# Output projection moved from the attention runs to a dense final stage of seven half-size products per pair of row tiles

## The chip, the cores and the metric

The kernel runs on one core of one Trainium2 chip. The metric is the device time of one execution in microseconds. A core has five engines, each working through its own instructions in order: TensorE (PE; its weight loads are listed apart as PEld), VectorE (DVE), ScalarE (ACT), GpSimd (POOL) and SyncE (SP). They are kept in step by semaphores. DMA transfers are issued from the instruction streams of SP, ACT and POOL; an issue whose data is not ready holds up everything behind it in that stream. Matrix products land in PSUM, eight banks of 128 x 512 fp32, from which DVE or ACT must take them before a bank can be written again.

## The reference

```python
def reference(A_x, A_k_cache, A_v_cache, A_wq, A_wo, B_x, B_w_gate, B_w_up, B_w_down):
    def _A_ref(x, k_cache, v_cache, wq, wo):      # 32 heads of 192, 2048 cached keys
        W = min(4096, max(256, Sk // 4))          # 512: the last 512 keys are used
        q = (x @ wq) as (B, Hq, Sq, Dh)
        k, v = the last W rows of k_cache, v_cache
        p = softmax((q @ k^T) * Dh ** -0.5)
        o = p @ v                                 # (B, Hq, Sq, Dh)
        return o as (B, Sq, Hq * Dh) @ wo         # 6144 -> 640
    def _B_ref(x, w_gate, w_up, w_down):          # F = 1536
        return (sigmoid(x @ w_gate) * (x @ w_up)) @ w_down
    xn = layernorm(A_x)                           # 2048 rows of 640
    s = _A_ref(xn, A_k_cache, A_v_cache, A_wq, A_wo)
    g = silu(_B_ref(xn, B_w_gate, B_w_up, B_w_down))
    return A_x + s * g
```

All inputs and the output are bf16. (Shortened to what is computed; `as` stands for the transposes and reshapes.)

## The kernel before

The order of every instruction on every engine is written out by hand, as the order of the statements of the program. It has two parts.

**The GLU** (L250 to L528) goes over the 2048 rows in four quarters s of 512. The f loop (L442) has twelve steps: ten products of gate and up into a double bank of PSUM (L449), the sigmoid on ACT (L454), the product with up on DVE into hT_sb (L455). Four double banks are used in turn (bank2, L79), so TensorE can be some tiles ahead of ACT and DVE. Then four row tiles q go through w_down (L495, products L499), with a sigmoid on ACT (L506) and a product on DVE (L507); the finished gate is stored to DRAM from POOL's queue (gB_d, L523). Layernorm, its transposes and sums of x stand between these steps.

Beside that the GLU stage finds a scale for wq: its 16 pieces are loaded (scan_load, L168), their magnitudes are folded into a running maximum on DVE (scan_fold, L177; L181 and L183). In quarter 2, at f = 6, set_scale (L185) reduces it on DVE (L186), writes the 128 numbers to DRAM (mx_d, L188) and reads them back into every partition (mx_row, L189), both from POOL's queue; at f = 11 set_scale2 (L191) makes the scale, a power of two. Quarter 3 then makes the query weights: scale_w (ACT: L219, copies L224) and sum_w (differences on DVE, L237 to L241). The query product is done by seven products in place of eight, on halves of 64 rows, in fp16 and bf16; that is what the scale and the sums are for.

**The runs** (loop L778): 16 runs r = (pi, g), where pi is a half of the rows (1024) and g a group of two pairs of heads (8 groups). Even runs have pi = 0, odd ones pi = 1. A run has

- 16 score tiles (stage_s, L647; products L655; exponential on ACT, L659), in two double banks, with the next run's query products between them (query_slots L573, q_after L776; products L565, copies on DVE L586, sums on DVE L603);
- 8 PV tiles (stage_pv, L661; products L673; DVE reciprocal L679, DVE product into o_st L680). Two of them fill one o_st, which SP's queue then transposes by DMA into oT (L686). There are two buffers of o_st (ost_pool, L535); in run 0 four slices of acc_lo stand in for them (L666), in run 15 there are four.
- after each PV tile one row tile of the output projection of the *previous* run (stage_wo, L738; wo_mm, L711; L716): six chunks of 128, each with 512 and with 128 columns, added on DVE to an fp32 sum acc (L747). With the last group the sum is multiplied by the gate, x is added, and the row tile is stored (finish, L722; gate and x are prepared on POOL, L708 and L709, as acc times gate plus x). The last run's eight projections come after the loop (L844).

k is loaded from POOL's queue (load_k, L131), scaled on DVE (L142) and transposed from SP's queue (L146); v is loaded from ACT's queue at the end of odd runs (L839), wo from ACT's queue (L556). The raw parts of wq come on POOL's queue (L202); their scaling and copies are on ACT, their differences on DVE, within PV of the even runs.

## Time and profile before

| | us |
|---|---|
| Median of 3 runs | 903.48 (903.33 to 903.51) |
| Profiled execution, span from the first to the last instruction | 901.5 |
| GLU, first quarter and its preparation, to 47.48 | 47.48 |
| GLU quarters 1 to 3 with their down parts, 47.48 to 164.30 | 116.82 |
| Query products of run 0, 164.30 to 175.64 | 11.34 |
| Run 0, scores, then PV, to 208.80 | 22.40, 10.76 |
| Runs 1 to 14, to 848.90 | 640.10 |
| Run 15 and the last projections, to 897.35 | 48.45 |
| After the last matmul | 4.15 |

The stage borders are read from the first and last instructions of each stage in the timeline. In the tables by stretch, a row gives the stretch, its length, then for each engine the busy time (and the number of instructions), the clock that TensorE was granted (1.00 is full), the share of time that the DMA engines were busy, and GB/s. In the page's second part, each digit is the busy share in tenths of one 40th of the span (22.5 us). In a group's line the two figures behind the bar are the busy time in all and the mean ns of one. In a line of the queue of an engine (POOL and SP among them), the bracket is the wait ahead of the instruction and what ended it.

### The profile page before, as it was taken

How to read it: one execution, taken by the hardware profiler on the slowest of the kernel's cores; microseconds unless marked ns; L12 is line 12 of the kernel's file. 1: busy time of each engine (PE TensorE's matmuls, PEld its weight loads, DVE VectorE, ACT ScalarE, POOL GpSimd, SP SyncE). 2: the span in 40 equal slices, each digit the busy share in tenths (PEclk: the TensorE clock that was granted, in tenths of full speed). 3: DMA queues.
4: the chain of work that ended last, by engine and by line, in shares of the span. 5: the costliest groups of instructions: out<-in, count | busy, mean ns of one | idle time of the engine just before them, and what ended most of it. 6: DMA issues, size and time to landing. Idle time of an engine off the chain costs nothing.

```text
span 901.5 us, 18561 instructions
## 1 busy us (share of the span) xinstructions
PE 895.3 (99%) x7791; PEld 531.9 (59%) x7791; DVE 652.5 (72%) x1093; ACT 432.9 (48%) x511; POOL 179.9 (20%) x222
## 2 busy tenths in 40 slices
PE   9999999999999999999999999999999999999998
PEld 5545454565656565656565656566666656565665
DVE  5879957777677866786778677866786678666567
ACT  4323346754247533753375437642854285424240
POOL 0051212771001100110011001100110000001983
PEclk9999999999999999999999999999999999999999
DMA  9993374415544545363626372727192715263745
GB/s 288 265 267 94 97 147 100 123 53 89 96 82 70 134 79 98 60 143 70 108 57 146 57 119 47 156 54 124 34 169 45 133 21 131 39 121 126 162 127 123
DMA packets 188357, 100.38 MB, mean 111 GB/s; under 512 B 156208, under 2 KB 180656, under 8 KB 188272
## 3 DMA queue, kind: packets, MB, share of 16 engines
q1 hardware_dynamic: 159088, 57.77, 32.1%
q0 software_dynamic: 9408, 29.93, 14.2%
q10 hardware_dynamic: 19776, 11.49, 5.4%
q8 instruction: 61, 1.00, 0.5%
q14 instruction: 24, 0.20, 0.1%
HBM read 57.87 MB, written 5.24 MB: 70 GB/s over the span
## 4 chain that ended last, share of the span: by engine, by line
PE 98%; DVE 1%; DMA 0%; ACT 0%; SPq 0%; issue 0%; POOL 0%; DVEq 0%
PE ps_all L716 23%; PE ps_all L565 20%; PE ps_all L673 19%; PE ps_all L655 18%; PE ps_all L449 11%; PE ps_all L499 6%; PE ps_all L362 1%; DMA x_sb<-in_A_x_dram 0%; ACT E L659 0%; DVE tmp L728 0%; DVE ps_all L725 0%; DVE o_sb L726 0%; SPq L297 0%; DVE stats L324 0%; POOL o_sb L729 0%
## 5 line engine op out<-in xcount | busy, mean ns | idle before, releaser
L659 ACT ACTIVATE E<-ps_all 128x1024 bf16<-128x1024 f32 x256 | 252.8, 1022 | 302.7 <-PE ps_all L655 279.0
L716 PE MATMUL ps_all<-wo_g,oT 128*128 128x512 bf16 (+2 forms) x1542 | 228.3, 299 | 0.0
L655 PE MATMUL ps_all<-qT,kT 64*128 64x512 bf16 x1536 | 194.3, 376 | 0.0
L673 PE MATMUL ps_all<-v_sb,E 128*128 128x193 bf16 x2048 | 189.8, 247 | 0.1
L673 PEld LDWEIGHTS <-E 128*128 128x128 bf16 x2048 | 168.6, 98 | 18.7 <-issue 6.8
L716 PEld LDWEIGHTS <-oT 128*128 128x128 bf16 x1542 | 122.0, 98 | 77.8 <-issue 2.1
L586 DVE COPY qp<-ps_all 128x512 f32<-128x512 f32 x150 | 100.8, 688 | 58.4 <-PE ps_all L565 58.4
L603 DVE TENSOR_TENSOR qT<-ps_all,qp 128x512 bf16<-128x512 f32 x165 | 109.7, 688 | 46.0 <-PE ps_all L565 39.4
L655 PEld LDWEIGHTS <-kT 64*128 64x128 bf16 x1536 | 75.3, 94 | 89.4 <-issue 5.2
L680 DVE TENSOR_TENSOR o_st<-ps_all,rden 128x768 bf16<-128x768 f32 x120 | 114.9, 957 | 5.0 <-DMA oT<-o_st 0.8
L202 POOL DMA_DIRECT2D raw<-in_A_wq_dram x80 | 48.0, 605 | 276.3 <-ACT wB L224 239.0
L135 POOL DMA_DIRECT2D k_sb<-in_A_k_cache_dram x32 | 32.7, 1027 | 270.6 <-DVE o_st L680 151.3
L219 ACT ACTIVATE raw<-raw,w_sc 128x1536 f16<-128x1536 bf16 x37 | 58.3, 1575 | 1.3 <-DMA raw<-in_A_wq_dram 0.4
L499 PE MATMUL ps_all<-wd_sb,hT_sb 128*128 128x512 bf16 (+1 forms) x384 | 52.8, 299 | 0.0
L565 PE MATMUL ps_all<-XB,wB 64*128 64x512 f16 x420 | 52.0, 376 | 0.0
L565 PE MATMUL ps_all<-X,w 64*128 64x512 bf16 x420 | 51.9, 376 | 0.0
L565 PE MATMUL ps_all<-XA,wA 64*128 64x512 f16 x420 | 51.9, 376 | 0.0
L747 DVE TENSOR_TENSOR acc_lo<-ps_all,acc_lo 128x640 f32<-128x640 f32 x48 | 39.5, 823 | 15.3 <-PE ps_all L716 15.0
L455 DVE TENSOR_TENSOR hT_sb<-ps_all,sig_sb 128x512 bf16<-128x512 f32 x48 | 32.4, 682 | 22.2 <-ACT sig_sb L454 11.5
L679 DVE RECIPROCAL rden<-ps_all 128x4 f32<-128x4 f32 x128 | 23.1, 181 | 33.5 <-PE ps_all L673 32.4
L454 ACT ACTIVATE sig_sb<-ps_all 128x512 bf16<-128x512 f32 x48 | 28.0, 596 | 40.1 <-PE ps_all L449 37.1
L747 DVE TENSOR_TENSOR acc_hi<-ps_all,acc_hi 128x640 f32<-128x640 f32 x48 | 39.3, 819 | 7.8 <-PE ps_all L716 7.8
(118 smaller groups left out, 764.4 us busy)
## 6 DMA issues: line engine op xcount, KB each, us to landing
raw<-in_A_wq_dram POOLq DMA_DIRECT2D x80, 192.0 KB, 3.8
k_sb<-in_A_k_cache_dram POOLq DMA_DIRECT2D x32, 192.0 KB, 5.8
wo_g<-in_A_wo_dram ACTq DMA_DIRECT2D x6, 960.0 KB, 6.9
v_sb<-in_A_v_cache_dram ACTq DMA_DIRECT2D x28, 192.0 KB, 3.7
gB_d<-gB_sb POOLq DMA_DIRECT2D x16, 160.0 KB, 4.1
gBa_sb<-gB_d SPq DMA_DIRECT2D x16, 160.0 KB, 3.7
xa_sb<-in_A_x_dram SPq DMA_DIRECT2D x16, 160.0 KB, 3.8
out_dram<-o_sb SPq DMA_DIRECT2D x13, 160.0 KB, 1.8
```

Source lines behind the costliest of these rows:

```text
L219: nc.scalar.activation(raw.bitcast(F16), raw, AF.Copy, scale=w_up)
L449: nc.tensor.matmul(gu[:, i, :], lhsT=w[:, c, f * P:(f + 1) * P], rhs=xnT[s][:, c, :], start=(c == 0), stop=(c == NCD - 1),)
L499: nc.tensor.matmul(oB_ps[:, d0:d0 + dsz], lhsT=hT_sb[:, f, q * P:(q + 1) * P], rhs=wd_sb[:, f, d0:d0 + dsz], start=(f == 0), stop=(f == NF ...
L565: nc.tensor.matmul(ps_all[:, b, :], lhsT=w(r, c), rhs=x[r, c, :], start=(first and k == 0), stop=(k == len(cs) - 1), skip_group_check=True,)
L586: nc.vector.tensor_copy(dst, part(b))
L603: nc.vector.tensor_tensor(q_out(i, u, pp), part(b), t, ALU.add)
L655: nc.tensor.matmul(ps[:, b, :], lhsT=kT[h, c * PC + j, :], rhs=qT_t[r][i, j][h, pp, :], start=(j == 0), stop=(j == PC - 1),)
L659: nc.scalar.activation(E_t[r, i, pp][:, c, :, :], ps, AF.Exp, scale=scale_qk)
L673: nc.tensor.matmul(o_ps[:, q // 2, q % 2, 0:DH + 1], lhsT=E[:, c, h, q * P:(q + 1) * P], rhs=vt[:, c, 0:DH + 1], start=(c == 0), stop=(c = ...
L680: nc.vector.tensor_tensor(o_st[:, :, h * DH:(h + 1) * DH].rearrange("p (b i) d -> p b i d", b=2), o_ps[:, :, :, 0:DH], rden[:].to_broadcas ...
L716: nc.tensor.matmul(oA[:, d0 - base:d0 - base + dsz], lhsT=oT_t[r, i, pp][:, q * PC + j, :], rhs=wo_t[runs[r][1]][:, cc, d0:d0 + dsz], star ...
L747: nc.vector.tensor_tensor(acc[t][:], oA[:, 0:D], acc[t][:], ALU.add)
```

## The change

The projection with wo leaves the runs. stage_wo, wo_mm, finish, load_wo, prepare and the pools for them are gone. Each transposed oT (384 KB) is stored to a DRAM array oT_d instead, from SP's queue (store_o), queued after the next transpose. After run 15 a final stage computes the whole projection. It takes the 6144 rows of wo as two halves h of 24 chunks; for each half and each of 8 pairs of row tiles (rows q of i = 0 and 1) it does seven products of half the size in place of eight (two by two blocks: row tile i, half of the 24 chunks, left or right 320 columns). So there are 16 steps m of 7 products of 12 matmuls with 320 columns, in fp16: 1344 matmuls, where there were 1542 of 512 or 128 columns. Each step loads its four quads (128 x 1536, 384 KB) two steps ahead from SP's queue, scales them on ACT, sums them on DVE (sum_quad), and takes the products out with three copies on ACT (keep) and four results on DVE (result), into acc for h = 0 and, with gate, acc and x, to the output for h = 1. The blocks of wo are loaded (load_ops), scaled on DVE (scale_op) and subtracted on POOL (sum_op): for h = 0 in runs 12 to 14, for h = 1 at m = 1 to 6. POOL prepares gate, acc and x at m = 7 to 14.

Two new scales are needed, for wo and for v. wo is scanned within the GLU: sixteen pieces of 480 KB, each loaded from POOL's queue into one of two buffers, its magnitude taken on ACT and folded on DVE one and two places later (wo_scan), at f 7, 9, 11 and q 1, 3 of quarter 1, f 1 to 11 and q 1, 3 of quarter 2, and f 1 to 9 of quarter 3. Its scale is set in the down part of quarter 3. v is scanned in the runs: magnitudes on ACT in the even runs, maxima on DVE (abs_v, max_v), the last four wholly on DVE in run 14, and its scale set in runs 14 and 15.

Several things move: the weight sums of the later groups go from DVE to POOL and their work is spread over PV of even and odd runs (weights); there are two sets of weight tiles and two k buffers; k is loaded at the start of even runs, and scaled and transposed at the first and fifth PV tile of odd runs; v is loaded from SP's queue; PV takes the banks in the order 0 1 2 3 2 3 0 1; run 15 puts its PV tiles between its score tiles; o_st has two buffers in every run, oT four.

```diff
+        wos_pool = bctx.enter_context(tc.tile_pool(name="wos_pool", bufs=2))
+        def wo_scan(n):
+            ok = range(HQDH // P // UC)
+            if n - 2 in ok and n > 2:
+                nc.vector.tensor_tensor(womax[:], womax[:], wos[n - 2][:], ALU.max)
+            if n in ok:
+                wos[n] = wos_pool.tile([P, UC, D], BF16, name="wos")
+                nc.gpsimd.dma_start(wos[n][:], wo_r[:, n * UC:(n + 1) * UC, :])
+            if n - 1 in ok:
+                nc.scalar.activation(womax[:] if n == 1 else wos[n - 1][:], wos[n - 1][:], AF.Abs)
...
+        wo_scan_at = [(1, f) for f in (7, 9, 11, 13, 15)] + [(2, f) for f in (1, 3, 5, 7, 9, 11, 13, 15)]
+        wo_scan_at += [(3, f) for f in (1, 3, 5, 7, 9)]
...
+                if (s, f) in wo_scan_at:
+                    wo_scan(wo_scan_at.index((s, f)))
                 if (s, f) in folds:
                     scan_fold(wmax, folds[s, f])
...
+                if (s, NF + q) in wo_scan_at:
+                    wo_scan(wo_scan_at.index((s, NF + q)))
+                if s == 3 and q == 0:
+                    set_scale(womax[:].rearrange("p c n -> p (c n)"), mx_row_o, mx_o, 1)
+                elif s == 3 and q == 3:
+                    set_scale2(mx_row_o, mx_o, o_up, o_down)
...
     def stage_pv(r, i, pp, h):
         if h == 0:
-            n, k = TQ * DH, i * G + pp
-            if r == 0:
-                ost_t[0] = lo_flat[:, k * n:(k + 1) * n].bitcast(BF16).rearrange("p (q d) -> p q d", q=TQ)
-            else:
-                ost_t[0] = (late["ost"] if r == last else ost_pool).tile([P, TQ, 2 * DH], BF16, name="o_st")[:]
+            ost_t[0] = ost_pool.tile([P, TQ, 2 * DH], BF16, name="o_st")[:]
...
             nc.sync.dma_start_transpose(oT[:], o_st.rearrange("p q d -> p (q d)"))
-            oT_t[r, i, pp] = oT
+            store_o()
+            oT_t.append((runs[r], i, pp, oT))
+
+    def store_o():
+        while oT_t:
+            (pi, g), i, pp, oT = oT_t.pop()
+            c = (g * G + pp) * PC
+            nc.sync.dma_start(
+                oT_d[pi][i][:, :, c:c + PC, :].rearrange("q p j e -> p q j e"),
+                oT[:].rearrange("p (q j) e -> p q j e", q=TQ),
+            )
...
+    def abs_v(g, n):
+        v = v_t[g, n // 2][n % 2][:, :, 0:DH]
+        a = vmax if (g, n) == (0, 0) else vabs_pool.tile([P, KC, DH], BF16, name="vabs")
+        vabs[g, n] = a
+        if g == NG - 1:
+            nc.vector.tensor_single_scalar(a[:].bitcast(I32), v.bitcast(I32), 0x7FFF7FFF, op=ALU.bitwise_and)
+        else:
+            nc.scalar.activation(a[:], v, AF.Abs)
+
+    def max_v(g, n):
+        if (g, n) != (0, 0):
+            nc.vector.tensor_tensor(vmax[:], vmax[:], vabs.pop((g, n))[:], ALU.max)
...
+            if r == last - 2 and 8 <= k < 12:
+                scale_op(0, (0, 4, 5, 3)[k - 8])
...
+            if pi == 1 and g < NG - 1 and k in (2, 4):
+                max_v(g, k // 2 + 1)
+            if (pi, g) == (0, NG - 1) and k in (6, 7, 8, 9):
+                abs_v(g, k - 6)
+                max_v(g, k - 6)
+            if (pi, g) == (0, NG - 1) and k == 9:
+                set_scale(vmax[:].rearrange("p c n -> p (c n)"), mx_row_v, mx_v, 2)
...
         for k, x in enumerate(pv_list):
+            if pi == 1 and g + 1 < NG and k in (0, 4):
+                scale_k((g + 1, k // 4))
+                turn_k((g + 1, k // 4))
             stage_pv(r, *x)
-            share = (k + 1) * len(wo_list) // len(pv_list)
-            while done < share:
-                stage_wo(*wo_list[done])
-                done += 1
...
+            if pi == 0 and g < NG - 1:
+                if k in (1, 2):
+                    abs_v(g, k - 1)
+                elif k in (4, 6):
+                    max_v(g, k // 2 - 2)
+            if pi == 0 and 1 <= g < NG - 1 and k in (3, 5):
+                weights(g + 1, 3 + k // 5)
+            if pi == 1 and g + 2 < NG and k in (1, 3, 5):
+                weights(g + 2, k // 2)
+        store_o()
+        if pi == 0 and g < NG - 1:
+            for n in (2, 3):
+                abs_v(g, n)
         if pi == 1 and g + 1 < NG:
             for pp in range(G):
-                load_v(g + 1, pp, nc.scalar)
+                load_v(g + 1, pp, nc.sync)
...
-    for i in range(2):
-        for q in range(TQ):
-            stage_wo(last, i, q)
+    for m in range(NP):
+        X, Y, Z = (4, 5, 6) if m % 2 == 0 else (0, 1, 2)
...
+        if m + 2 < NP:
+            load_quads(m + 2)
+        if m == 1:
+            load_ops(1)
+        elif m == 2:
+            for n in (0, 4, 5, 3):
+                scale_op(1, n)
+        elif 3 <= m < 7:
+            sum_op(1, m - 3)
+        if 7 <= m < NP - 1:
+            prep_load(m + 1)
+            prep(m + 1)
+        product(m, Y, "S1", 1, True)
...
+        keep(Y, p5s)
+        product(m, X, "S2", 2, False)
...
+        product(m, Z, "A12", 3, True)
+        result(m, 0, LEFT, Z, p1s)
...
+        product(m, X, "S3", 4, False)
+        result(m, 1, RIGHT, X, p5s)
...
+            product(m + 1, 4 - X, "A11", 0, True)
+            keep(4 - X, p1s)
+        product(m, Y, "S4", 5, False)
+        result(m, 0, RIGHT, Y, u2s)
+        product(m, X, "A22", 6, False)
+        result(m, 1, LEFT, X, None)
```

Here product() is twelve matmuls of 320 columns, keep() a copy on ACT, and scale_quad and sum_quad (left out above) put A21, A11, A22, A12 on ACT and the four sums of the next step on DVE. POOL's part in a step with h = 1 is prep(): gate times the scales, acc times gate, plus x, for both row tiles.

## The prediction

> **What bounds the kernel now.** I read the page's totals and slices first, then its chain, then the stages one by one.
>
> ```profile
> PE 895.3 (99%) x7791; PEld 531.9 (59%) x7791; DVE 652.5 (72%) x1093; ACT 432.9 (48%) x511; POOL 179.9 (20%) x222
> ...
> DVE  5879957777677866786778677866786678666567
> ...
> PE ps_all L716 23%; PE ps_all L565 20%; PE ps_all L673 19%; PE ps_all L655 18%; PE ps_all L449 11%; PE ps_all L499 6%; PE ps_all L362 1%; DMA x_sb<-in_A_x_dram 0%; ACT E L659 0%; DVE tmp L728 0%; DVE ps_all L725 0%; DVE o_sb L726 0%; SPq L297 0%; DVE stats L324 0%; POOL o_sb L729 0%
> ```
>
> TensorE is the bound and never waits; the output projection (L716) is 23% of the chain. But VectorE is at 9 tenths in slices 3 and 4, inside the GLU, where this change adds work. By stage (columns: stretch, length, then busy time of PE, PEld, DVE, ACT, POOL):
>
> ```profile
> 73.38:86.42 13.04, 13.04 (x97) 7.39 (x96) 12.22 (x18) 3.17 (x5) 1.69 (x3) 1.00 0.52 135
> 86.42:112.32 25.90, 25.90 (x121) 11.72 (x120) 23.73 (x38) 9.79 (x15) 6.47 (x10) 1.00 0.37 93
> ...
> 125.36:151.26 25.90, 25.90 (x121) 11.72 (x120) 18.24 (x32) 18.92 (x28) 6.27 (x9) 1.00 0.68 148
> ```
> ```profile
> 198.04:208.80 10.76, 10.76 (x129) 10.60 (x129) 9.09 (x16) 0.97 (x1) 6.35 (x9) 1.00 0.61 100
> 208.80:848.90 640.10, 640.10 (x5952) 389.55 (x5952) 464.85 (x779) 320.43 (x358) 76.87 (x94) 1.00 0.49 93
> 848.90:897.35 48.45, 48.45 (x424) 30.39 (x422) 31.75 (x48) 15.30 (x16) 32.43 (x24) 1.00 0.54 143
> ```
>
> The down part of GLU quarter 1, the f loop of quarter 2 (DVE 92%) and that of quarter 3; then run 0's PV alone (10.76), runs 1 to 14 (45.72 each), run 15 with the last projections.
>
> **The saving.** A row tile of L716 takes 1.63 us in the chain (12 matmuls of 320 columns in the mean: 0.136 each). Eight leave each of runs 1 to 14: 45.72 - 13.04 = 32.68, times 14 is 457.5. Run 15 alone: 16 score tiles at 0.68, PV 10.76, and 1.7 because its first five score tiles now run at the pace of the exponential (1.0 each, L659) with nothing between: 23.4. The final stage: 16 x 7 x 12 matmuls at 0.136 = 182.8. With 4.15 after the last matmul: 208.8 + 457.5 + 23.4 + 182.8 + 4.15 = 876.7, 24.8 below the profiled span of 901.5 (the fp16 and bf16 forms of L565 both take 376 ns, so the type costs nothing). Everything below is added to 876.7.
>
> **The scan of wo in the GLU.** Sixteen POOL loads of 480 KB (those of XA: 4.8 us to landing), 16 Abs of 128x1920 on ACT (from 1575 ns for 1536 and 521 for 384: 0.915 ns an element, so 1.93 us) and 15 maxima on DVE (L183: 1.16). Each engine works in order, and on ACT each Abs stands among the sigmoids and waits for its load; behind it wait the sigmoids, then hT on DVE, then TensorE, which can be three tiles ahead. There are two wos buffers, so load n also waits on POOL until DVE has taken maximum n-2.
>
> ```profile
> 105.09 2.10 DVE L186 TENSOR_REDUCE w_sc<-wmax 128x1 f32<-128x1920 bf16 x1
> ...
> 114.02 0.68 DVE L455 TENSOR_TENSOR hT_sb<-ps_all,sig_sb 128x512 bf16<-128x512 f32 x1
> ```
> ```profile
> 107.49 0.59 POOL L188 DMA_DIRECT2D mx_d<-w_sc  x1 [13.30 <-DVE w_sc L186]
> 115.02 0.56 POOL L189 DMA_DIRECT2D mx_row<-mx_d  x1 [6.95 <-DMA mx_d<-w_sc]
> ```
> ```profile
> 110.78 1.28 ACT L454 ACT_TABLE_LOAD   x1
> 112.07 1.08 ACT L454 ACTIVATE sig_sb<-ps_all 128x512 bf16<-128x512 f32 x2
> ```
>
> Quarter 2: TensorE starts the down products at 112.15 and needs the last hT at 115.1; it comes at 114.70, 0.4 before. The set of the query scale (f 6) keeps POOL 7.5 us between mx_d and mx_row. Behind it now queues wo load 8 (f 7), and Abs 8 stands on ACT ahead of the table load and the sigmoids of f 10 and 11. Five maxima (5.8) come ahead of the reduction on a DVE with no gap there: mx_row 115.0 + 5.8 = 120.8; load 121.4, landed 126.2; Abs to 128.1; table and two sigmoids to 130.5; last hT 131.2. That is 16 us late for a need at 115.1; I take +16. Low end without the 5.8: +10. High, if loads land in 6.6 us, as those of XC: +18.
> By the Trainium skill (DMA: Bandwidth & Descriptors, section Anatomy of one DMA — SWDGE (gpsimd) path) such a write has a fixed cost of about 2 us; mx_d here took 7.2. By the rule this term would be about 11.
>
> Quarter 3: ACT holds 18.92 plus four waits of 1.4 to 1.9 for DVE's weight sums, 25 of 25.9. Abs at f 1 and 3 fall into such waits; those at f 5 and 7 don't (3.86); maxima stand ahead of the sums at f 1, 3 and 9 (3.5). 7.3 less 0.9 of slack: I take +7 (low 0.7, the busy sum 18.92 + 7.72 against 25.9; high 10, if loads hold it too).
>
> wo's scale: L186's 2.1, mx_d 7.5, mx_row 4.2 after the first of the last four down tiles: DVE waits in set_scale2 until about 17 us after that tile's end, ahead of the first query sum, whose bank TensorE wants at 13.0: with the sum's 0.69, +4.5 (2 to 7).
>
> **PV without cover.** In run 0 of the trace PV runs dense and VectorE keeps up, but there o_st is four slices of acc_lo. Now it has two buffers in every run, so the fifth product waits for the first transpose.
>
> ```profile
> 198.04 10.83 PE L673 MATMUL ps_all<-v_sb,E 128*128 128x193 bf16 x128
> ...
> 202.21 9.32 SPq L686 DMA_TRANSPOSE oT<-acc_lo  x4
> ```
> ```profile
> oT<-o_st SPq DMA_TRANSPOSE x60, 4.6
> ```
>
> Counted from PV's start: transpose 0 issued 4.2, landed 8.8; product 4 (7.1 in run 0) ends 9.8, product 5 11.0; transpose 1, issued 6.8, landed 11.4; product 6 ends 12.5. The next run's first query slot wants that bank at 12.06: +0.5 for each of eight runs, 4 in all (landing 3.7: none; 7.0: 2.9 each, 23). In the seven even runs two maxima over v (0.56, from L183's slope) move product 6 to 12.9 and the second maximum to 13.5. The fourth Abs waits for it (two buffers), and ACT runs Abs (0.87) ahead of the next run's exponentials: the first ends at 15.4, and the third score tile, due at 13.1, starts at 15.5: +2.4 each, 17 (10 to 33 by the same landings).
>
> **Covered, or small.** The stores queue behind the next transpose on SP, and the v loads, moved from ACT's queue to SP's, behind the stores; v is needed 15 us later, at the next PV: 0. If that cover went, PV would start late. The stores add 1.57 MB a run; the queue of wo and v (q10) took 48.7 us (5.4% of the span) for 11.49 MB, so about 6.6 us; the DMA engines' 22.4 us a run (0.49 of 45.72), less 2 for wo, become 27 of 32.7: busy, not full. Weight sums on POOL (L237 to L241: 4.2 a chunk, two or three a run): 0. K loads now start in the even run, 25 us ahead of use: 0. In run 13 DVE scales half of wo (four of 128x3840, some 1.2 each by L142's 0.63 for 1536), in run 14 it takes v's last four magnitudes and maxima (4.5); both stand between query sums whose banks TensorE wants again within 2.4 us: +4 (0 to 8, nearly all of the 9.3). In the final stage a pair takes TensorE 84 x 0.136 = 11.4; ACT scales four quads and keeps three products, 4 x 1.58 + 3 x 0.44 = 7.6; DVE takes four sums of 128x1536 (0.96 by L183's slope) and from pair 8 on eleven ops of 128x320 (0.41 to 0.53, L725 and L726), about 9: TensorE leads; at pair 2 DVE waits for the second half of wo behind 1.6 MB of quads: +1.5 (0 to 8). From pair 8 DVE's ops with two SBUF inputs (7.0) meet POOL's 7.6; in run 0 a meeting cost L221 0.23 (0.84 for 0.61). Some eleven a pair are 2.5, just the slack: +5 (0 to 22, if the two never overlapped: 3.2 x 7).
> The Trainium skill (SBUF — State Buffer, section Who interferes with whom) says that they never do: the port pair is locked for a whole instruction. This rule would make it the 22; the row, 0.23, is the nearer.
>
> **Sum.** 876.7 + 16 + 7 + 4.5 + 4 + 17 + 4 + 1.5 + 5 = 935.7; the runs' median stands 2.0 above the profiled span: **938 us**.
>
> **Rivals.** Covered: TensorE works up to three tiles ahead of ACT and DVE, and the scan hides as the query scan does now. For it: not one wait of TensorE inside the GLU. Against it: 0.4 us of slack in quarter 2. All low ends but quarter 2's and the v maxima at nil: 876.7 + 2 + 4 = 883, **faster**; it decides if the added stalls stay under 24.8.
> Late transposes: landings of 7.0 and 8.3 us occur before, beside K loads; at 7.0 the PV terms become 23 + 33: 973. Against: now K loads run outside PV, stores behind.
> The change not done as said: 1344 products of 320 columns are counted in the code; if their pace were that of 98 ns loads plus stream (0.15), 938 + 19 = 957.
>
> **Chances.** Forecast 0.58 (own range 912 to 958); late transposes or slow products 0.14; between the forecast and no change 0.06; covered 0.18 (883, and up to 901 as the low ends are left); within 0.2% (what the measurement can tell from none) 0.04. So faster 0.18, same 0.04, slower 0.78. The range 889 to 962 leaves out the lower half of the covered case and the upper half of the late one, about a tenth on each side.
>
> **What would show it.** In the profile after: waits of PE L449's line and its down products in quarters 2 and 3 for DVE or ACT, 20 to 30 us in all; ACT's Abs waiting on wos loads; DVE's o_st waiting on DMA; score tiles of odd runs waiting for ACT; a final stage of 183 to 190 us with PE dense. Wrong, if PE shows no waits in the GLU, or if the final stage has the largest ones.

## The result: 1034.8 us against a forecast of 938

| | before | after |
|---|---|---|
| Median, us | 903.47 (4 runs, 903.33 to 903.51) | 1034.82 (4 runs, 1029.68 to 1039.98) |
| Span of the profiled execution | 901.5 | 1027.9 |
| TensorE busy | 895.3 | 908.7 |
| Mean granted clock of TensorE | 1.0 | 0.959 |

The changed kernel is slower by a ratio of 1.1454 (95% interval 1.1408 to 1.1500). Slower was forecast, but by 35 us, not by 131; the time lies outside the range of 889 to 962. The profiled execution is the shortest of the four.

First the page of the changed kernel: busy time by engine, then its 40 slices for TensorE and for the clock that it was granted.

```profile
PE 908.7 (88%) x7593; PEld 571.4 (56%) x7593; DVE 727.0 (71%) x1086; ACT 574.7 (56%) x633; POOL 420.2 (41%) x410
...
PE   9999577699989989889899999896989966999886
...
PEclk9999979999999999999999999998999877999989
```

TensorE, busy 99% of the span before, now stands idle for 119 us (1027.9 less 908.7). A slice is 25.7 us: the deep holes are in slices 5 to 8 (the GLU and the query products), 28 (run 13), 33 and 34 (the final stage) and 40, with shallow ones through the runs between, and the clock dips below 9 tenths in four of the deep ones (6, 28, 33 and 34). By stage (columns as in the tables of before) the GLU, the query products of run 0, run 15 and the final stage; then, in a second table, runs 1 to 12 and runs 13 and 14.

```profile
0.00:197.51 197.51, 166.81 (x985) 83.30 (x985) 139.22 (x227) 98.98 (x121) 45.02 (x68) 0.97 0.68 183
197.51:217.00 19.49, 14.85 (x107) 6.43 (x107) 8.99 (x18) 8.33 (x14) 16.98 (x25) 0.82 0.40 98
...
767.20:791.15 23.95, 23.12 (x224) 14.67 (x224) 17.38 (x33) 15.61 (x16) 0.23 (x1) 1.00 0.55 150
791.15:1023.40 232.25, 198.26 (x1347) 135.88 (x1344) 165.63 (x183) 107.74 (x108) 122.34 (x52) 0.91 0.48 154
```
```profile
250.20:684.22 434.02, 403.15 (x3950) 263.93 (x3949) 300.17 (x492) 291.29 (x318) 178.27 (x225) 0.98 0.72 146
684.22:767.20 82.98, 69.42 (x661) 45.09 (x662) 69.83 (x92) 33.53 (x35) 34.33 (x10) 0.96 0.73 180
```

Laid beside the forecast's base of 876.7, every stage can be booked. A run without stalls takes 32.84 us here (12 x 32.84 = 394.1; 2 x 32.84 = 65.7).

| Stage | measured | base | excess | forecast of the excess |
|---|---|---|---|---|
| GLU | 197.5 | 164.3 | 33.2 | 23 (16 + 7) |
| Query products, behind wo's scale | 19.5 | 11.3 | 8.2 | 4.5 |
| Runs 1 to 12 | 434.0 | 394.1 | 39.9 | 21 (4 + 17) |
| Runs 13 and 14 | 83.0 | 65.7 | 17.3 | 4 |
| Final stage | 232.2 | 182.8 | 49.4 | 6.5 (1.5 + 5) |
| Pace of 32.84 for 32.68, run 15, the end | | | 3.2 | 0 |

The excess is 151.2, and 876.7 + 151.2 = 1027.9, the span. No stage is missing from the forecast's list; the sizes are wrong, and those of the runs and of the final stage by far.

**The GLU and the scale of wo.** Timeline of ACT, POOL, DVE and TensorE; the bracket is the wait and what ended it.

```profile
115.88 0.57 POOL L201 DMA_DIRECT2D mx_d<-w_sc  x1 [5.31 <-DVE hT_sb L484]
...
123.20 0.55 POOL L202 DMA_DIRECT2D mx_row<-mx_d  x1 [6.75 <-DMA mx_d<-w_sc]
123.76 1.49 POOL L295 DMA_DIRECT2D wos<-in_A_wo_dram  x2
...
130.27 1.80 ACT L297 ACTIVATE wos<-wos 128x1920 bf16<-128x1920 bf16 x1 [10.88 <-DMA wos<-in_A_wo_dram]
...
134.77 0.71 PE L528 MATMUL ps_all<-wd_sb,hT_sb 128*128 128x512 bf16 x2 [14.03 <-DVE hT_sb L484]
...
203.77 0.29 DVE L205 TENSOR_REDUCE w_sc<-mx_row_o 128x1 f32<-128x128 f32 x1 [3.87 <-DMA mx_row_o<-mx_d]
...
205.51 8.11 PE L588 MATMUL ps_all<-mid 64*128 64x512 f16 x49 [4.11 <-DVE qT L622]
```

This is the chain that the prediction drew: the scale's return (mx_row) holds POOL, the wo load behind it is issued at 123.76, its Abs starts at 130.27, and the last hT reaches TensorE 14.03 us late. Down to the single steps the forecast was within a few us: mx_row at 123.2 (120.8 forecast), Abs done at 132.1 (128.1).

**The runs.** In the trace, every even run from 2 to 12 begins with a wait of 2.5 to 4.2 us at the query products, because o_st of the odd run before waits for transposes; the odd runs wait 0.6 to 1.0 for ACT, and runs 1, 7 and 11 some 1.2 more for o_st. Run 3 handing over to run 4:

```profile
362.73 0.96 DVE L695 TENSOR_TENSOR o_st<-ps_all,rden 128x768 bf16<-128x768 f32 x1 [5.42 <-DMA oT<-o_st]
...
363.74 1.80 PE L588 MATMUL ps_all<-mid 64*128 64x512 bf16 x10 [3.92 <-DVE o_st L695]
```

**GpSimd's subtractions.** In run 13 (7.11 us of TensorE waiting) and in the final stage's steps 4 to 6 one thing is seen: short DVE instructions that last as long as a GpSimd subtraction of 128x3840.

```profile
704.14 7.43 POOL L725 TENSOR_TENSOR arm<-mid,arm 128x3840 f16<-128x3840 f16 x1 [17.18 <-DVE mid L720]
704.58 9.14 DVE L720 TENSOR_SCALAR mid<-mid,w_sc 128x3840 f16<-128x3840 bf16 x2
...
714.37 1.44 PE L588 MATMUL ps_all<-mid,arm 64*128 64x512 bf16 x5 [7.11 <-DVE qT L622]
...
807.37 0.95 DVE L799 TENSOR_TENSOR mid<-mid 128x1536 f16<-128x1536 f16 x1
...
835.30 8.23 POOL L725 TENSOR_TENSOR op<-op,arm 128x3840 f16<-128x3840 f16 x1
836.97 7.39 DVE L799 TENSOR_TENSOR mid<-mid 128x1536 f16<-128x1536 f16 x1
...
843.50 16.24 POOL L725 TENSOR_TENSOR op<-op,op 128x3840 f16<-128x3840 f16 x2
844.39 8.07 DVE L801 TENSOR_TENSOR mid<-mid 128x1536 f16<-128x1536 f16 x1
844.41 3.38 PE L916 MATMUL ps_all<-arm,mid 128*128 128x320 f16 x12 [3.96 <-DVE mid L799]
```

The sum at L799 takes 0.95 us with GpSimd idle and 7.39 beside the subtraction; it ends at 844.36, when the subtraction of 835.30 has passed (843.53), not when its own work is done.

**The clock.** Twelve matmuls of L916 take 3.38 us there, 1.63 when dense. The table by stretch; the clock is the third figure from the end. First the stretch of 2 us from 1.5 us after a wait of 2.79 us (start of run 2), then the one after a wait of 2.99 (start of run 12), then a wait of 3.9 in the final stage and the matmuls behind it:

```profile
293.00:295.00 2.00, 2.00 (x12) 0.86 (x10) 1.15 (x2) 0.94 (x1) 1.92 (x3) 0.50 1.18 267
```
```profile
652.60:655.00 2.40, 2.33 (x22) 1.25 (x23) 2.01 (x5) 0.39 (x1) 2.18 (x4) 1.00 1.16 282
```
```profile
840.50:844.40 3.90, 0.00 (x0) 0.00 (x0) 3.87 (x2) 0.00 (x0) 3.90 (x2) 0.50 0.00 0
844.40:847.80 3.40, 3.38 (x12) 1.64 (x12) 3.40 (x1) 0.00 (x0) 3.40 (x1) 0.50 0.00 0
```

Behind the waits of 3.9 us and more TensorE gets half its clock for some us; behind waits of 2.5 to 3.0 it was granted 1.00 in runs 8, 10 and 12, and 0.50 in run 2. So a long wait is paid twice: once in waiting, once in the matmuls behind it. What decides can be read in the trace's record of the clock. It changes only on a grid of periods of 3.41 us. In this kernel a full-clock period in which TensorE stands idle for 2.16 us or more is followed by one at half clock, and one with 1.97 or less is not (over all kernels here the border lies between 1.8 and 2.1). The wait of 2.79 has 2.27 us in one period; that of 2.99 falls on two, with 1.35 and 1.64. The Trainium skill (TensorE: Matmul & The Clock Gate, section Why this matters for your kernels) asks for no idle gap over about 3 us between bursts; the waits of 3.9 us and more agree, the one of 2.79 shows that a shorter one can be enough.

The last kernel below runs the same 7593 matmuls (by the records) with hardly a wait in 874.5 us of busy time, 34 us less than the 908.7 here. TensorE was busy for 55.6 us at half clock, which accounts for about 28 of the 34; the rest is not explained. All of it lies inside the excesses of the table.

### The profile page after: what moved, and what is told of

Its sections match the earlier page's. It is cut to its first block, busy times and chain, and to the rows that moved or that the text cites. A ratio compares the mean times of both kernels' runs of the same rounds, so it can differ in the third digit from the quotient of the medians.

```text
span 1027.9 us, 18854 instructions
## 1 busy us (share of the span) xinstructions
PE 908.7 (88%) x7593; PEld 571.4 (56%) x7593; DVE 727.0 (71%) x1086; ACT 574.7 (56%) x633; POOL 420.2 (41%) x410
## 4 chain that ended last, share of the span: by engine, by line
PE 50%; DMA 15%; DVE 11%; issue 6%; POOL 3%; ACT 3%; SPq 0%; DVEq 0%; POOLq 0%; ACTq 0%
PE ps_all L588 16%; PE ps_all L674 13%; PE ps_all L916 11%; DMA oT<-o_st 9%; PE ps_all L688 8%; DVE o_st L695 2%; DMA wos<-in_A_wo_dram 2%; DMA arm<-gB_d 1%; DVE mid L799 1%; DVE mid L801 1%; DVE vmax L740 1%; POOL acc L909 1%; DMA mid<-in_A_wo_dram 1%; POOL arm L908 1%; ACT E L678 1%
## 5 line engine op out<-in xcount | busy, mean ns | idle before, releaser
L688 PEld LDWEIGHTS <-E 128*128 128x128 bf16 x2048 | 170.8, 98 | 15.9 <-issue 14.3
L916 PEld LDWEIGHTS <-mid 128*128 128x128 f16 x996 | 100.6, 102 | 73.1 <-DVE mid L799 16.0
L588 PE MATMUL ps_all<-mid,arm 64*128 64x512 f16 (+1 forms) x840 | 109.4, 386 | 21.2 <-DVE o_st L695 11.1
L588 PE MATMUL ps_all<-mid 64*128 64x512 f16 (+1 forms) x840 | 108.6, 386 | 16.9 <-DVE o_st L695 12.2
L588 PEld LDWEIGHTS <-arm 64*128 64x128 f16 x840 | 48.0, 96 | 69.4 <-issue 27.6
L588 PEld LDWEIGHTS <-mid 64*128 64x128 f16 x840 | 48.5, 96 | 65.2 <-issue 24.5
L916 PE MATMUL ps_all<-arm,mid 128*128 128x320 f16 x348 | 58.6, 326 | 23.2 <-DVE mid L799 14.0
L250 POOL TENSOR_TENSOR arm<-mid 128x384 f16<-128x384 f16 x20 | 18.3, 916 | 120.4 <-ACT mid L232 101.8
L789 ACT ACTIVATE mid<-mid,w_sc 128x1536 f16<-128x1536 bf16 x41 | 63.4, 1568 | 1.4 <-DMA mid<-oT_d 1.3
L232 ACT ACTIVATE mid<-mid,w_sc 128x1536 f16<-128x1536 bf16 x37 | 58.1, 1571 | 0.6
L528 PEld LDWEIGHTS <-hT_sb 128*128 128x128 bf16 x384 | 30.0, 99 | 46.5 <-DVE hT_sb L484 20.1
L218 POOL DMA_DIRECT2D mid<-in_A_wq_dram x80 | 48.6, 612 | 11.4 <-DVE mid L254 11.4
```

The lines of the kernel that those rows point to most:

```text
L218: eng.dma_start(raw[r], wq_r[:, c, :, g * GC:(g + 1) * GC])
L232: nc.scalar.activation(raw.bitcast(F16), raw, AF.Copy, scale=w_up)
L528: nc.tensor.matmul(oB_ps[:, d0:d0 + dsz], lhsT=hT_sb[:, f, q * P:(q + 1) * P], rhs=wd_sb[:, f, d0:d0 + dsz], start=(f == 0), stop=(f == NF ...
L588: nc.tensor.matmul(ps_all[:, b, :], lhsT=w(r, c), rhs=x[r, c, :], start=(first and k == 0), stop=(k == len(cs) - 1), skip_group_check=True,)
L688: nc.tensor.matmul(o_ps[:, q // 2, q % 2, 0:DH + 1], lhsT=E[:, c, h, q * P:(q + 1) * P], rhs=vt[:, c, 0:DH + 1], start=(c == 0), stop=(c = ...
L789: eng.activation(t, t.bitcast(BF16), AF.Copy, scale=v_up)
```

## The experiments

Each kernel is the changed kernel with one edit where nothing else is said, profiled once, until the combined ones. Spans and stage lengths are compared; repeated runs of the changed kernel lie up to 10.3 us apart, so only differences above that, or in a single stage, are read.

**1. Is it the scan of wo that holds the GLU?** The scan and its scale are left out.

```diff
-                if (s, f) in wo_scan_at:
-                    wo_scan(wo_scan_at.index((s, f)))
...
-                if s == 3 and q == 0:
-                    set_scale(womax[:].rearrange("p c n -> p (c n)"), mx_row_o, mx_o, 1)
-                elif s == 3 and q == 3:
-                    set_scale2(mx_row_o, mx_o, o_up, o_down)
```

> The scan of wo is left out of the GLU; its scale is a constant power of two, the value that the scan finds for these inputs. My theory: the scan alone costs the GLU its 33 us and the first query products their 8 us, by the waits for ACT and DVE and by the half clock that follows the long ones. Then the GLU ends at 164 to 166 us (197.5 with the scan), the first score tile starts at 175 to 177 (217.0), no clock below 1.00 is granted before that, and the time falls by 38 to 42 us, to 988 to 1000. Rival: other moves (later k loads, weight tiles shared with other data, a cold clock by itself) carry part of it: the GLU still ends after 172.

Measured 997.71 us. The GLU ends at 164.31, as before the change (164.30), and the scores of run 0 start at 176.69 for 217.0. The excess of the first two stages, 40 us of 41, is the scan. (The span falls by 32 only: the stages behind came out 8 us longer in this run, 7 of them in runs 1 to 14.)

**2. What makes the transposes late in odd runs?** Four edits. My theory was that the transposes of k, put between those of o on SP's queue, make o_st wait:

```diff
+            if pi == 1 and g + 1 < NG and k in (12, 13):
+                scale_k((g + 1, k - 12))
+                if k == 12:
+                    turn_k((g + 1, 0))
...
-            if pi == 1 and g + 1 < NG and k in (0, 4):
-                scale_k((g + 1, k // 4))
-                turn_k((g + 1, k // 4))
+            if pi == 1 and g + 1 < NG and k == 0:
+                turn_k((g + 1, 1))
```

> The k tiles of the next group are scaled at score tiles 12 and 13 of the odd runs and transposed at score tile 12 and ahead of PV, not within PV. My theory: in the odd runs' PV the second k transpose and the stores stand on SP's queue between the transposes of oT, so that the oT of the first pairs land 7 to 9 us after their issue and VectorE waits 4.3 to 5.7 us for an o_st buffer; without the k transpose these waits fall under 1 us, as in the even runs' PV, runs 2 to 12 of even number go from 35.5 to 41.8 us to about 33.7 each, and the time falls by 15 to 24 us. Rival: two o_st buffers are too few whatever else is in the queue, or the stores alone delay the landings: the waits stay above 3 us and the time falls by less than 6 us.

Measured 1045.87: the theory fell. The o_st waits of even runs stay (3.0 to 4.9 us), and run 13's PV grew to 25.4 because the scaling of k now stood behind a GpSimd subtraction. A third buffer instead:

```diff
-    ost_pool = lctx.enter_context(tc.tile_pool(name="ost_pool", bufs=2))
+    ost_pool = lctx.enter_context(tc.tile_pool(name="ost_pool", bufs=3))
```

> Three o_st buffers in place of two, the k transposes left where they are. My theory: the seventh product waits for the first transpose in place of the fifth, 2.7 us more of cover against waits of 4.3 to 5.7: waits of 1.5 to 3 us are left at the seventh product, and the next run's query products are reached in time in most runs; the time falls by 12 to 22 us. Rival: the queue itself is late (each transpose waits for the one before), so a later product waits as long as the fifth did: less than 6 us.

Measured 1011.4, 23 us less; runs 1 to 12 take 420.8 us for 434.0. The waits for o_st are gone from them, but waits of 0.5 to 5.2 us for kT stand in the even runs instead: the third buffer moves part of the wait along SP's queue, so the transposes themselves are late, whoever waits for them. The stores, held until the end of PV, were the next suspect:

```diff
             nc.sync.dma_start_transpose(oT[:], o_st.rearrange("p q d -> p (q d)"))
-            store_o()
...
-            (pi, g), i, pp, oT = oT_t.pop()
+            (pi, g), i, pp, oT = oT_t.pop(0)
```

> The four stores of oT of a run are issued after its PV, not between its transposes. Two theories of the late oT landings in odd runs (9.4 us where even runs have 3.7, with the k transposes in the way or moved ahead): by the first, a transpose that follows a store on SP's queue waits for the store (its issue takes 6.4 us there and 1.4 us elsewhere), so that now the waits for o_st fall under 0.5 us and the time falls by 15 to 22 us; by the second, the DMA engines' own time is short (in a window of 22 us around an odd PV: 7680 packets of 256 B of the transposes, 10.9 us over 16 engines, the loads of wq 6.1, the stores 1.8 of some 5), and taking out the stores helps only in part: 5 to 12 us.

Measured 1041.74, o_st waits 3.2 to 4.5 us in the even runs: not the stores. What is left beside the transposes are the raw loads of wq. With the work on the weights, the diff moved three of five pairs of them into PV of the odd runs; here they are issued among the score tiles of the next run:

```diff
-            load_raw(n // NCD, n % NCD, nc.gpsimd)
+            raw_later.append((n // NCD, n % NCD))
...
+            if k in (3, 5, 7) and raw_later:
+                load_raw(*raw_later.pop(0), nc.gpsimd)
```

> The loads of wq parts (two in an even, three in an odd PV, from GpSimd's queue) are issued at score tiles 3, 5 and 7 of the next run in place of within PV. By the theory that the DMA engines' time is short in odd PV, taking 6.1 us of packets out of it helps as much as taking out the stores: o_st waits of 1 to 2 us in place of 2.5 to 4.2, 6 to 12 us faster. By the theory that stores hold up the transposes on SP's queue it changes nothing there: within 3 us of 1030 to 1040.

Measured 997.87, 32 us less in the span. Runs 1 to 12 in the table by stretch (to be laid beside 434.02 above), and TensorE's waits for o_st between 250 and 720 us, first of the changed kernel (total, number, longest), then with the loads moved:

```profile
249.33:652.28 402.95, 396.95 (x3949) 255.48 (x3949) 299.41 (x492) 291.62 (x318) 181.73 (x225) 1.00 0.72 157
```
```profile
PE ps_all L588 <- DVE o_st L695: 23.0, 9, 4.2
```
```profile
PE ps_all L588 <- DVE o_st L695: 3.2, 4, 1.6
```

The six even runs from 2 to 12 now take 32.8 to 33.3 us. What the loads do is seen in the DMA issues of one odd PV (run 3, 22 us from its start): number of issues, and the median from issue to landing. The changed kernel, then with the loads moved:

```profile
mid<-in_A_wq_dram POOLq DMA_DIRECT2D x6, 192.0 KB, 6.6
...
oT<-o_st SPq DMA_TRANSPOSE x4, 7.4
```
```profile
oT<-o_st SPq DMA_TRANSPOSE x4, 3.6
```

A transpose lands in half the time. In that stretch the changed kernel's trace has 7680 packets of 256 B for the transposes and, for wq, 64 packets of 3072 B and 128 of 4608 B, the latter of 661 ns each in the mean.

Is it their queue, GpSimd's, or the DMA engines that they load? One kernel puts the loads on ACT's queue:

```diff
-            load_raw(n // NCD, n % NCD, nc.gpsimd)
+            load_raw(n // NCD, n % NCD, nc.scalar)
```

> The loads of wq parts stay within PV, where the oT transposes are late, but are issued from ScalarE's hardware queue, not from GpSimd's software queue. e6 showed that these loads, not the stores and not the k transposes, make the oT land late in odd runs. If it is their packets on the DMA engines (4608 B each, 661 ns in the mean there, ahead of transposes' packets of 256 B and 23 ns), the o_st waits of even runs stay at 2.5 to 4.2 us and the time at 1025 to 1040. If it is the software queue (GpSimd writing its descriptors, while it does the weight sums), they go as in e6, and the time falls to 995 to 1010.

Measured 1102.78, and it decides nothing: a load on ACT's queue waits for the buffer that GpSimd's weight sums free, and ACT's exponentials wait behind it, 4 to 9 us in most runs. So another kernel takes experiment 6 and adds six spare loads of wq to each odd PV, from ACT's queue, into memory that nobody reads, so that they wait for nothing:

```diff
+                spare = arm[:, NW + k // 2 * 2 * GC:NW + (k // 2 + 1) * 2 * GC].rearrange("p (h n) -> p h n", h=2)
+                for rr in (LO, HI):
+                    nc.scalar.dma_start(spare[rr], wq_r[:, k // 2, :, g * GC:(g + 1) * GC])
```

> As e6 (the wq loads moved out of PV, 998 us), with six loads of the same parts of wq put back into the odd runs' PV, into memory that nobody reads, from ScalarE's hardware queue and waiting for nothing; so the DMA engines carry the same bytes there as before e6, but GpSimd writes no descriptors. If the loads hold up the transposes on the DMA engines themselves, the o_st waits of 2.5 to 4.2 us come back in the runs of even number and the time is 1015 to 1035. If it was GpSimd's software queue, the runs stay at 32.8 to 33.3 us and the time at 996 to 1003.

Measured 1026.69. Run 3's PV, and the waits between 250 and 720 us:

```profile
arm<-in_A_wq_dram ACTq DMA_DIRECT2D x6, 192.0 KB, 4.2
...
oT<-o_st SPq DMA_TRANSPOSE x4, 7.1
```
```profile
PE ps_all L588 <- DVE o_st L695: 13.0, 9, 3.1
```

The transposes are back at 7.1 us and o_st waits again, without GpSimd's queue in it: it is the loads themselves. Whether they hold the transposes up in the DMA engines or in the memory behind them is not shown. (The spare loads came as packets of 1536 B, and v and k landed later as well, so the 29 us that they cost are not the same 32.)

**3. GpSimd's subtractions.** All eight on DVE, or all eight still on GpSimd but in twelve pieces of 128x320:

```diff
-        nc.gpsimd.tensor_tensor(a, b, c, ALU.subtract)
+        nc.vector.tensor_tensor(a, b, c, ALU.subtract)
```

> The eight subtractions over 128x3840 of the wo blocks are done on VectorE in place of GpSimd. My theory: VectorE and GpSimd exclude each other for whole instructions, so that each of the GpSimd subtractions (7.4 to 8.3 us) stops VectorE's next instruction with two SBUF operands until it ends; on VectorE one takes about 2.4 us (0.95 for 1536 columns), the stall of TensorE from 831 to 863 us is gone (25 us, half clock counted), and in run 13 the two k scalings of 4.6 and 3.5 us take 0.6 again; less some 2.4 us for each of the three sums in runs 13 and 14 where it is not hidden: the time falls by 25 to 35 us. Rival: VectorE was short of time there anyway, or waited for the wo loads: less than 12 us.

```diff
-        nc.gpsimd.tensor_tensor(a, b, c, ALU.subtract)
+        for k in range(KB):
+            nc.gpsimd.tensor_tensor(a[:, k, :], b[:, k, :], c[:, k, :], ALU.subtract)
```

> The eight subtractions over 128x3840 stay on GpSimd, cut into twelve of 128x320 each (about 0.66 us each by the 7.4 to 8.3 us of the whole). If the exclusion of VectorE lasts for a whole GpSimd instruction, VectorE's sums now wait at most 0.7 us for one piece, the stall of TensorE from 831 to 863 us nearly vanishes, run 13 loses its 7.1 us wait and its long k scalings, and the time falls by 28 to 40 us, as much as with the sums on VectorE or more. If the two share the port by cycles, the total is what matters: VectorE's sums still take 2 to 3 times 0.95 us while GpSimd is at it and at most 10 us come back.

The final stage took 207.2 us and 208.8 for 232.2 (1004.05 and 1006.19 in all); run 13 44.5 and 37.9 for 46.1. The same sums in the timeline, first with the subtraction (L725) on DVE, then beside twelve pieces on GpSimd (7 and 12 of them in a line):

```profile
834.82 2.15 DVE L725 TENSOR_TENSOR arm<-op,arm 128x3840 f16<-128x3840 f16 x1
...
840.55 0.95 DVE L799 TENSOR_TENSOR k_sb<-mid 128x1536 f16<-128x1536 f16 x1
```
```profile
839.86 11.87 POOL L726 TENSOR_TENSOR op<-op,arm 128x320 f16<-128x320 f16 x12
...
842.24 1.43 DVE L802 TENSOR_TENSOR mid<-k_sb,kT 128x1536 f16<-128x1536 f16 x1
```

Beside pieces a sum takes 1.43, beside whole subtractions 7.4 to 8.1: here DVE waits for about the one GpSimd instruction that it meets. And the work was on the wrong engine: 2.15 us on DVE, 8.2 on GpSimd.

That settles the final stage, but not run 13. With the subtractions on DVE runs 13 and 14 take 81.6 us for 83.0, with pieces 73.7. In run 13 the four scalings (1.2 each), a wait of 1.85 for the last block of wo and now two subtractions (4.34) stand on DVE ahead of a query sum, and TensorE waits 6.63 us for it, where it waited 7.11; with pieces on GpSimd it waits 2.49. So there the trouble seems to be how much work of 128x3840 stands at one place in DVE's order, whether DVE does it or waits for it; in the last kernel below, which spreads it over runs 13 to 15, run 13 takes 33.2.

The 24 us that the final stage still lost were taken on in one step: the subtractions on DVE, the buffers of the kept products moved out of the way of the first quads, and the gate's scaling from GpSimd to ACT.

```diff
-            nc.gpsimd.tensor_scalar(gate, gate, descale, None, op0=ALU.mult)
+            nc.scalar.activation(gate, gate, AF.Copy, scale=descale)
...
+    cp_pool = ctx.enter_context(tc.tile_pool(name="cp_pool", bufs=1))
+    p1s, p5s, u2s = (cp_pool.tile([P, DN], F32, name=n) for n in ("p1s", "p5s", "u2s"))
```

> Three edits of the final stage at once, each in its own place: the subtractions on VectorE (as in e4: 207 us for the stage in place of 232); the buffers of the three copies no longer in memory that the last stores of oT still read, so that ScalarE's first copy doesn't wait for them (4.5 us of wait and 3 us of half clock at the start); and the gate scaled on ScalarE instead of GpSimd (2.2 us of GpSimd's 5 for a row tile), with its load a step earlier. My theory of the rest (GpSimd and VectorE meeting in the last eight steps, VectorE waiting for GpSimd's acc): 186 to 193 us for the stage, no stall over 2 us in it. Rival: DVE or the loads are too slow in the last eight steps by themselves: still over 198 us.

Measured 990.26; the final stage 198.1, at the 198 of the rival and not the 186 to 193 of the theory. The start wait of 4.5 us is gone, but three waits of 2.2 us in the last eight steps remain, where GpSimd's acc times gate and plus x (1.4 to 2.1 us each) still meet DVE's sums (2.1 for 0.95).

**4. Does the projection pay once its stalls are gone?** Four kernels combine the edits. Common to them: three o_st buffers; wq loads late; the scales of wo and v taken from sums of magnitudes, which ACT's Abs accumulates, so that DVE's maxima go (a bound on the largest magnitude, not the maximum itself); the second half's subtractions on DVE, the first half's in pieces on GpSimd; acc times gate plus x made on the first eight steps of the final stage.

```diff
-                nc.gpsimd.dma_start(wos[n][:], wo_r[:, n * UC:(n + 1) * UC, :])
...
-                nc.scalar.activation(womax[:] if n == 1 else wos[n - 1][:], wos[n - 1][:], AF.Abs)
+                nc.scalar.dma_start(wos[n][:], wo_r[:, n * UC:(n + 1) * UC, :])
...
+                nc.scalar.activation(a, a, AF.Abs, accum_out=l1[:, n - 2:n - 1])
...
+        nc.scalar.activation(vabs[:], v, AF.Abs, accum_out=l1_v[:, 4 * g + n:4 * g + n + 1])
```

> All that the experiments showed, in one kernel, with nothing left out of the computation. wo's and v's scales come from sums of magnitudes that ScalarE collects as it takes them (no maxima on VectorE, no buffer that waits for it), wo's pieces loaded from ScalarE's queue, its scale set in runs 1 and 2; the wq loads issued in the next run's scores; three o_st buffers; the wo blocks of the first half scaled at four score tiles of runs 13 and 14 and subtracted on GpSimd in pieces, those of the second half on VectorE in steps 4 to 7; the copies' buffers moved; the preparation of gate, acc and x in steps 1 to 8, not 7 to 14. By the theory of the stages: GLU to 165, query products 11.4 to 12.4, run 0 33.1, runs 1 to 12 at 32.9, 13 and 14 at 34, run 15 24, final stage 186 to 192: a span of 885 to 897, that is 887 to 899 against 903.5. If something new stands in its way (ScalarE's sums cost more, GpSimd and VectorE collide in steps 1 to 8): 900 to 915.

Measured 923.5, above all that was expected. Runs 1 to 12 stood at 32.8 to 34.2, but the GLU ended at 173.9, the final stage lost 7.3 us to one wait, and run 15 took 36.87 for the same trouble in another form: GpSimd's pieces back to back let a DVE product of 128 numbers wait for 19.59 us, until two rows of twelve pieces were through.

```profile
681.37 9.00 POOL L726 TENSOR_TENSOR arm<-mid,arm 128x320 f16<-128x320 f16 x12
688.71 19.59 DVE L810 TENSOR_TENSOR w_sc<-w_sc 128x1 f32<-128x1 f32 x1
690.34 8.99 POOL L726 TENSOR_TENSOR mid<-mid 128x320 f16<-128x320 f16 x12
699.30 8.97 POOL L726 TENSOR_TENSOR mid<-mid,arm 128x320 f16<-128x320 f16 x12
```

The second spreads the pieces and puts a quarter of them back on DVE, moves that product to ACT, takes v's scale through SP's queue, and loads v ahead of the last stores and wo earlier in the GLU:

```diff
-            nc.vector.tensor_tensor(descale, v_down, o_down, ALU.mult)
+            nc.scalar.activation(descale, v_down, AF.Copy, scale=o_down)
...
-                set_scale(l1_v[:], mx_row_v, mx_v, 2)
+                set_scale(l1_v[:], mx_row_v, mx_v, 2, nc.sync)
```

> b1 with its remaining stalls taken away: wo's pieces at f 0 to 7 of quarters 1 and 2 and in the down part of quarter 1 only (b1 lost 9 us, most of it in quarter 3 behind the pieces of the down part before it); the next v loaded ahead of the last stores of oT (v waits of 1 us in four runs, 2.5 us in run 14); the one product of two scales that stood 19.6 us on VectorE behind GpSimd's pieces made on ScalarE, the pieces in run 13, the last subtraction on VectorE; v's scale through SP's queue; two sets of rows for the preparation, loaded a step ahead of ScalarE (a stall of 7.3 us). By the same sum as for b1: GLU 164.3 to 168, queries 12.4, run 0 33.1, runs 1 to 12 394, 13 and 14 67, 15 24, final stage 184 to 188, tail 4: a span of 883 to 891, a time of 885 to 893, 1 to 2 per cent under the kernel before. If a new stall comes in the place of an old one: up to 905.

Measured 915.16 (914.70 to 917.43), ratio 1.0133 (1.0116 to 1.0150). The final stage took 183.66, the forecast's dense 182.8, and runs 1 to 12 their 32.84; what was left was the GLU (181.9, Abs waiting up to 6.9 us for wo on full DMA engines) and run 15 (34.57, o_st behind the scale on SP's queue). The third loads only half of wo in the GLU and the rest in the runs, and puts v's scale back on GpSimd's queue:

```diff
-            ok = range(HQDH // P // UC)
+            ok = range(8)
...
+            if (r, k) == (0, 0):
+                for n in range(3):
+                    wo_load(8 + n)
+            elif r in (1, 3, 5, 7, 9) and k == 2:
+                wo_load(11 + r // 2)
```

> b2 with the three stalls that were left. In b2 the wo pieces of quarter 1 were loaded while the DMA engines were full (263 to 334 GB/s) and ScalarE waited up to 6.1 us for one, so the GLU ended at 181.9: now eight pieces in the GLU (from f 8 of quarter 1 to f 7 of quarter 2) and eight in the PV stages of runs 0, 1, 3, 5, 7 and 9, where ScalarE is idle or nearly so. Run 15 took 34.6 us because v's scale went through SP's queue and pushed the quads' loads into the oT transposes (an o_st wait of 8.2 us): back on GpSimd's queue, with the subtractions behind it. Run 13 lost 2.7 us to three scalings of wo blocks: now two. If these are the causes: GLU 165 to 168, query products 12.4, run 0 33.1, runs 1 to 12 394, run 13 33 to 34, run 14 33 to 34.5, run 15 24 to 26, final stage 183.7, tail 4: a span of 883 to 890 and a time of 885 to 892, below the kernel before. If the GLU's loss is not the loads but ScalarE's sums themselves, the GLU still ends after 173.

Measured 896.87 (895.36 to 899.98), ratio 0.9935 (0.9912 to 0.9958). Two collisions were left: run 10 at 40.73 us, its v landing behind stores and loads of k and wq, and run 15 at 26.89, where a DVE subtraction of 128x3840 took 10.90 us behind GpSimd's pieces, 2.15 otherwise. The last takes those away and nothing else:

```diff
-        if h == 1 or n == 3:
+        if h == 1 or n >= 2:
...
-            if r == last and k == 4:
-                sum_op(0, 3)
+            if r == last and k in (1, 3):
+                sum_op(0, 2 + k // 2)
...
-        if pi == 0 and g + 1 < NG:
-            for pp in range(1 if g == 0 else 0, G):
-                load_k((g + 1, pp))
+        if r == 0:
+            load_k((1, 1))
...
+            if pi == 0 and g + 1 < NG and g > 0 and k == 10:
+                for pp in range(G):
+                    load_k((g + 1, pp))
```

> b3_all with two edits: the k loads of the next even head are issued at score tile 10 of the even runs instead of behind the stores, and the last two of the first half's weight subtractions run on VectorE instead of GpSimd. Theory (what is left over the forecast are two collisions: run 10's 40.73 us with a v wait of 5.6 behind loads, and run 15's 26.89 with a VectorE sum of 10.90 behind back-to-back GpSimd pieces): run 10 falls to about 32.8 (-7.9), run 15 to 24.0-24.8 (-2 to -3), the span of 894.6 to 883-888 and the time to 885-890. Rival (the transfers are only moved onto others, so that another run waits as long): one of runs 0 to 14 shows a new wait of 3 us or more and the time stays at 893-899.

Measured 889.37 (5 runs, 888.44 to 890.40), ratio 0.9845 (0.9831 to 0.9859): 1.5% less than before, and 145 us less than the change as it was made. Its page, and its stages (GLU; runs 1 to 14; run 15; final stage):

```profile
PE 874.5 (99%) x7593; PEld 548.7 (62%) x7593; DVE 666.7 (75%) x1041; ACT 593.3 (67%) x702; POOL 330.0 (37%) x394
```
```profile
0.00:166.44 166.44, 162.76 (x987) 82.91 (x987) 122.56 (x212) 85.86 (x121) 34.90 (x57) 1.00 0.77 197
...
211.93:675.78 463.85, 461.00 (x4607) 291.82 (x4607) 342.27 (x557) 339.35 (x394) 199.48 (x253) 1.00 0.86 175
675.78:699.64 23.86, 23.01 (x226) 14.71 (x226) 20.32 (x32) 15.68 (x17) 2.51 (x4) 1.00 0.69 158
699.64:883.30 183.66, 182.89 (x1346) 131.32 (x1344) 147.57 (x188) 118.36 (x124) 56.59 (x32) 1.00 0.64 209
```

Its span of 887.2 stands 10.5 above the forecast's base of 876.7, and 6.4 of that is in runs 1 to 14. TensorE is dense again, with a clock of 1.00 in each of these stages. So 14.3 of the 24.8 us of saving are reached, and of the 151 us of excess all but 10 were stalls that the products themselves don't need.

## Why the prediction was wrong

**Right.** The direction, and the saving: 24.8 against the profiled span was worked out, 14.3 are realised in the last kernel. The final stage's dense time (182.8; 183.66), run 15 (23.4; 23.9) and the pace of a run (32.68; 32.84) hold to within about 2%. The chain through the GLU was right.

**GLU, 23 forecast, 33.2 measured; wo's scale, 4.5 and 8.2.** The mechanism was right. The waits alone are 28.8 us in the GLU (33.2 less 4.4 of slower matmuls: TensorE was busy for 166.81 rather than 162.37) and 4.1 ahead of the query products, where 4.5 was forecast. Quarter 2 with its down part waits 18.0 us (16 forecast), quarter 3 9.6 (7). The rest is slower matmuls: 4.4 us in the GLU, and 49 matmuls in 8.11 us behind the wait of 4.11, at a clock of 0.50 for the first 5 us or so. The prediction had no term for the clock anywhere.

**PV without cover, 4 for o_st and 17 for v's maxima; 39.9 measured in runs 1 to 12.** Here two terms were wrong in opposite ways. The 17 was mostly absent: the odd runs lose 11.8 in all, but wait only 0.6 to 1.0 us for the exponential, 4.8 in six of them (3.7 more are waits for o_st in runs 1, 7 and 11), as the even runs' transposes landed earlier than taken (3.6 us for 4.6 in run 2), and the second maximum with them. And the 4 became 28: the six even runs lose 28.3 in all (waits for o_st 19.3, for v 3.0, the rest slower matmuls). The failed step is "now K loads run outside PV, stores behind", with which the rival of late transposes was put down to 0.14. That sentence looked at k and at the stores and not at the third stream: the wq loads, of which the diff moves three pairs of five into the odd runs' PV, beside the k transposes and the stores. The trace of before had shown this stream at work. The prediction put landings of 7.0 and 8.3 down to K loads; the 7.0 has K loads beside it, but the 8.3 and the other four of 8.0 to 9.3 have loads of wq and of wo, and no K load. The last transpose of run 6, for example, with the other issues between 480 and 497 us (number, size, us to landing):

```profile
wo_g<-in_A_wo_dram ACTq DMA_DIRECT2D x1, 960.0 KB, 7.6
raw<-in_A_wq_dram POOLq DMA_DIRECT2D x2, 192.0 KB, 6.0
oT<-o_st SPq DMA_TRANSPOSE x1, 8.7
```

The rival's landing (7.0 us) is what was measured in the changed kernel (7.4), but its 973 is not the time, since all that it adds to the forecast is in PV.

**Runs 13 and 14, 4 and 17.3; final stage, 6.5 and 49.4.** The failed step is "this rule would make it the 22; the row, 0.23, is the nearer". The rule (the Trainium skill, SBUF — State Buffer, section Who interferes with whom) has a DVE instruction with two SBUF inputs and a GpSimd instruction that reads SBUF shut each other out for a whole instruction. Here is the meeting behind the 0.23, in the timeline of the kernel before:

```profile
177.06 0.50 POOL L239 COPY acc_hi<-raw 64x384 f16<-64x384 f16 x1
177.14 0.84 DVE L221 TENSOR_SCALAR raw<-raw,w_sc 128x1536 f16<-128x1536 bf16 x1
177.65 1.10 POOL L240 TENSOR_TENSOR acc_hi<-raw,acc_hi 128x384 f16<-128x384 f16 x1
```

DVE met a copy of 0.50 us of which 0.42 was left, so this meeting could not have cost much more than its 0.23, whatever the rule: it says nothing against it. (L221 is also a product with a column of scalars, not a sum of two tensors.) At the new sizes the trace shows 0.95 become 7.39 beside 8.23, and 1.43 beside pieces of 0.99 (11.87 for 12). In these meetings the cost goes with the length of the GpSimd instruction, and the row should have been scaled by it. Even the 22 would have missed most of it, since it priced only the meetings with POOL's gate work; the eight subtractions of 128x3840 that the change puts on POOL have no price against DVE in it at all. The four of them in the final stage are 25.0 of its time (232.2 to 207.2 with them on DVE). Of the other 24.4, the three edits of the start and the gate took 9.1 away, and nearly all of the rest was gone in the combined kernels, which make the gate work in steps 1 to 8 (183.66) but differ in more than that; which meeting costs what there was not told apart. In runs 13 and 14 the 4 was the price of the scalings and of v's magnitudes alone. The subtractions that follow the scalings at the same place in run 13 had none, and there moving them to DVE gives back 1.4 us of the 17.3, cutting them into pieces 9.3; the rest stays open.

**The range.** Its lower part rested on a case in which the scan hides, its upper on late transposes; no case took the high ends of several stages together, none had a price for the subtractions on POOL, and none had the clock in it, though matmuls took 34 us more beside 119 us of idle TensorE. A slip: the low ends that the covered case names add 2.7 us, so that it stands at 881 rather than 883.

**What was to show it.** PE waits in quarters 2 and 3 for DVE and ACT of 20 to 30 us: 27.6. "Wrong, if PE shows no waits in the GLU, or if the final stage has the largest ones": in sum it does (34.0 us of idle TensorE, for 30.7 in the GLU), though the longest single wait, 14.03 us, is in the GLU.

## What to carry to other kernels

When work moves to GpSimd, ask how long a single instruction of it is and how many run back to back, not only how long the work is: short VectorE instructions on the critical path waited for a whole one here (7.39 us for 0.95), and once for some 24 pieces (19.59). When a change moves loads as a side effect of moving the work that uses them, list every stream that now runs beside the transfers that set the pace; six loads beside the transposes doubled the landing here, and the trace of before had landings of 8 to 9 us in such company. And where a forecast holds waits that leave TensorE idle for 2 us or more of a 3.41 us period, add the half-clock stretch behind each.
